# A DeltaNet and MLP-mixer kernel: every step issued in another order, with 32 products of zeros for 25

## The chip, the cores and the metric

The kernel runs on one core of a Trainium2 chip. The metric is the device time of one execution in microseconds. Before the change the median of three runs is 651.53 us (650.95 to 651.62).

## The reference

Attention in DeltaNet form for 4 batches of 8 heads, 768 time steps and head size 48, followed by an MLP mixer over time and over channels. All is fp32.

```python
k_n = k / (np.linalg.norm(k, axis=-1, keepdims=True) + 1e-06)
for t in range(S):                       # S = 768, state is D x D per batch and head
    y[:, :, t] = einsum('bhd,bhde->bhe', q[:, :, t], state)
    v_old = einsum('bhde,bhd->bhe', state, kt)
    state = state + bt * einsum('bhd,bhe->bhde', kt, vt - v_old)
# x = y as (B, S, H*D) = (4, 768, 384)
h = np.maximum(x.transpose(0, 2, 1) @ w_tok1, 0.0) @ w_tok2    # 768x256, 256x768
u = x + h.transpose(0, 2, 1)
h2 = np.maximum(u @ w_ch1, 0.0) @ w_ch2                        # 384x1536, 1536x384
return u + h2
```

## The kernel before, in words

The 768 time steps of a batch are cut into chunks of 64. A chunk is solved in closed form: the products of its keys with each other give a 64x64 triangle per head, the triangle is inverted, and the state is carried from chunk to chunk with a few products. Two chunks form a unit: 24 units u, six for each batch, 48 chunks t = 2u and 2u + 1. All work is written as Python generators, called jobs, that issue a few instructions at each step. A string named `order` lists the steps: `i0*3` means three more steps of job i0. Nothing is scheduled behind it: each engine runs its instructions in the order in which the string issues them, and waits only where an operand or a buffer is not ready. SyncE starts all the DMAs, also in that order, so a DMA that has to wait for a buffer holds back those after it.

The jobs, with a number for the unit, the round, the chunk, the batch or the piece of weights:

- w0 to w33 (`round_weights`, `round_pair`) bring in a piece of weights: step 1 is the load (L273), step 2 two ScalarE operations (L279, L280), step 3 a VectorE shift (L282), step 4 a GpSimd addition (L286). The loads share three buffers in turn, so the load of a piece waits for the GpSimd addition of the third piece before it in the list. From w22 on every second piece adds differences of weights (L301).
- k (`load_kq`) loads a unit's keys and queries, v (`load_v`) its values (last step on GpSimd, L416), b the factors beta.
- p (`prep`) scales keys and turns keys and queries on TensorE (L488, L507; from unit 12 on VectorE instead).
- c and d (`grams`) make the 64x64 products (L442) and scale them on VectorE (L445).
- t (`to_parts`) hands the 32x32 blocks on the diagonal to a round, i (`invert`) inverts a round's blocks on VectorE in some thirty small steps (L663, L668), f (`from_parts`) hands them back. Round 0 is units 0 to 3, round 1 is units 4 and 5, later rounds are four units each. Rounds 0 and 1 work on blocks of 16: L677 transposes, ScalarE (L678) and VectorE (L679) mask the two sides, L684 transposes again. From unit 6 on the blocks pass through DRAM.
- h (`join_16`, units 0 to 5) joins quarters of 16 to 32: products L701, scaling on ScalarE (L707), products L716. The first of these steps clears a buffer z on GpSimd (L543). j (`join`) joins 32 to 64: a VectorE transpose (L740), products L764, ScalarE copies (L769), products L751.
- r (`recur`) is one chunk of the recurrence: p_k on TensorE (L804), `rest` on VectorE (L811, step 5 where the state is not empty), p_y and p_w (L824, L828), a ScalarE copy (L834), p_s and p_y (L842, L843), the new state on VectorE (L851).
- m (`mixer`) is one batch of the mixer: six steps of token products (L1000), six of p_h with their additions on VectorE (L1013, L1017), then channel products (L1080 for batch 0, L972 with differences of weights for the others; L1102). s (`sum_weights`) makes those differences.
- x, z and Y (`keep_warm`, `warm_tiles`, L227 and L237) multiply zeros into a bank that nobody reads: x is 128 columns, z is 512, Y is four small ones. fp32 products take two passes on TensorE, so the profile counts each of x and z twice.

Of the kernel before, what the change touches and what calls it, by code (L numbers as in the profile page):

```python
# [23 lines left out]
def kernel(  # L24
# [1165 lines left out]
    r4*2 w16*3 p7*4 r4*2 p7 r4 j3*5 w16 p9 i1 r5*5 d7*3 w5 d7*2 c7 r5*2 c7*4 w5  # L1190
    k10*2 t6 r5*2 w5 r6*4 v3*3 w27 v3 Y v3 r5 w27 i1 w27 t6 p8*2 v4 p8*2 p7 w24*3 z
    h5*5 h4*2 r6*3 p8*2 i1 h4*3 v4 f4*2 r6*3 k11 w27 c8*5 d8*5 t7 p8 t7*2 r7*5 t7
    f4 w26*3 h4*3 p9 w26 h4 v4 h4*3 p9 j4 h4 r7*2 w24 p9*4 r7*2 p9 d9*2 p10*2 c9 f5
    c9 p9 d9*3 t6*2 r8 c9*3 Y w28 r8 j4 w28 j4*2 r7 j4 v4*2 t8*4 w4 m0 w28*2 j4*5
    w4*2 p10 f5*2 r8*2 j4 r8 h5 w27*2 w7*3 r8*2 h5*3 r8*2 w7 r9*2 h5*4 r9*2 r8 j5
# [7 lines left out]
    t10*3 r12*3 f9*2 j8*2 r13*2 j8 r13*3 w25 m0 f9*2 r13 p11 r13 p12*2 r13*2 p11  # L1203
    d11 p11 c11 w20*3 c11*2 d11 w25 c11*2 w20 d11*3 t10 p12 w30 w32*2 r14*2 w32*2
    r14 p12 r14*2 r13 v8*3 m0*3 r14 d12 v8 r14 w30*3 v8 k13*2 c12 d12 c12 w29 d12
    k13*2 w23 k13*6 c12*3 p12 d12*2 r14*2 k13 t11 k13 r14 t11 m0*3 j9 r15*4 p13*3
    m0 r15*3 p13*4 t12 w33 m0*2 t12*3 r15*3 d13 c13*2 d13*2 c13*3 d13*2 m0*3 w31*2
    j9 r16*2 j9 k14*4 r16*2 w33*4 j9*3 r16 m0 w33 w31 w33 m0 k14 r16*2 j9*3 w23*2
    r16 m0 r16 r17*2 k14*3 p14*2 t11*2 t13*4 i3 j9 v10*2 k14 p14 r17*2 r16 r17
    p14*2 k15*4 m0 v9 m0 p14 p13 v9*2 m0 i3*3 w25 v9 k14 i3 m0*2 i3 m0 i3*5 r17 k15  # L1210
    k14*2 m0*2 k15 m0*2 i3*4 r17 i3*2 r17*3 i3*6 j9 i3*2 p14 k15*2 m0*5 v9 v10
    k15*4 i3 r18*5 i3*6 m0 v10 m0 v10 m0*9 r18 d14 r18 c14 p14 d14 c14 d14*2 p15
    c14 p15*2 r18*2 m0*3 r19 c14*2 r18 f13 r19*2 f10*2 r19 p15*2 r19 m0*5 r19*2 f10
    j10 f10 f11*4 j10*2 s j10*3 j11 r19*2 d14 m0*2 k16 j11 r20*2 j11 k16*6 j11
    r20*2 j11 p15 f12 p15*2 r20 r19 t14 f12*2 k16*5 v11*2 f13*2 m0 j11 m0 r20*2
    d15*2 p16 c15 r20*3 d15 c15*3 p16*2 v11*2 c15 d15*2 t15 r21*5 p16*2 k17 m0*3
    r21 k17*2 j12*2 r21*4 p16 j12*4 j13 s r22*3 v11 r22 m0*2 r22*2 m0 p16*2 d16 r22
    c16 r22 c16 d16*3 k17 r22 c16*2 k17*7 p17*3 k17 c16 p17 r23*2 v12*4 r23*3 r22
    m0 d16 t16*2 p17 r23 p17 t16 r23 p17*2 t15*3 m0*2 t14 m0 d17 c17*3 d17 c17 d17
    s c17 d17 r23 d17 t16 s*4 m0*4 s*3 m0*3 t14 m0*3 s t14 m0 t17*4 f12 k18*2 i4*2  # L1220
    j13*2 k18*2 r23 k18*3 i4*6 j13*2 v14*2 m0*3 i4*2 m0 j13 v12 r24*2 f13 j13 r24*2
    m0 v14*2 i4*3 r24*3 k18*2 i4 k18*2 p18*2 i4 m0 i4 m0*2 i4 p18*2 i4 j13 r25*2
    j13 r25*2 p18 k19*5 r24 j13 k19*3 i4*2 m1*5 r25*2 k18 i4*2 r25 i4*4 v13*2 i4
    v13 i4 v13 m1 j13 r25*2 m1 v13 i4*4 p19 m1 p18*3 k19*4 r25 m1*2 r26*3 f16 r26
    p19*2 m1 r26 m1*3 s r26*2 c18 d18 c18 d18*2 p19 m1*3 r26*3 m1*3 f14 m1*2 r27*2
    c18 r27*3 p19 f14*3 c18 d18*2 m1*2 j14 r27*2 c18 m1 r27 j14*2 f15*2 p19 j14*3
    m1*2 p19*2 f15*2 j15*2 r27 r28*2 j15 v14 f16*2 s r28*3 j15 r27 j15 j16 k20 s*3
    j15 m1*2 k20 m1 k20*10 m1*2 r28*2 d19 c19*2 d19 c19 d19 c19 d19*2 r28*2 c19 t18
# [19 lines left out]
    r42*2 j22 m2*4 j22 m2*3 r43*2 f22 r43 r42 r43 m2*3 r43 m2*12 f23 m2*3 r43 m2
    r43 j23 m2*2 r43*3 j23*3 r44*3 j23*2 r44 v22*2 r44 m2*5 r44*2 m2*3 r44*3 m2*3
    f23 m2*4 r45 j23 r45*3 j23*3 r45*3 m2*7 r45 v23 m2*4 v23 m2*2 v23 m2*2 v23  # L1250
# [39 lines left out]
```

## Time and profile before

| what | value |
|---|---|
| median of 3 runs | 651.53 us |
| profiled execution, its own time | 652.18 us |
| its span, first to last instruction | 650.4 us |
| TensorE busy | 619.6 us (95%) |
| VectorE busy | 446.4 us (69%) |
| ScalarE busy | 259.6 us (40%) |
| GpSimd busy | 108.6 us (17%) |
| mean granted TensorE clock | 0.976 |
| DMA | 50.25 MB, 75 GB/s of HBM traffic over the span |

Times in the views are microseconds from the span's start. PE is TensorE, PEld its weight loads, DVE VectorE, ACT ScalarE, POOL GpSimd, SP SyncE. A row of the timeline has the start, the duration, the engine, the line, the operation, output and inputs, and in brackets the engine's idle time before it and what ended it. Digits of the page's second part are busy shares of 40 equal slices in tenths.

### The profile page before, as it was taken

What the parts mean: (1) busy time and instruction counts of PE and PEld (TensorE: products, weight loads), DVE (VectorE), ACT (ScalarE), POOL (GpSimd) and SP (SyncE); (2) the same over time, 40 slices, a digit from 0 to 9 for tenths busy, and PEclk for the clock granted to TensorE, in tenths of its full rate; (3) what the DMA queues carried; (4) which work ended last, traced back from release to release, by engine and by line L of the source; (5) the groups of instructions that cost most, each with busy time, mean ns of one, the idle gap of its engine ahead of it and who ended that gap; (6) DMA issues with size and microseconds to landing.
All of it is one profiled execution on the core that took longest, in us unless ns stands there. A gap on an engine that the chain in (4) does not pass through costs nothing.

```text
span 650.4 us, 21453 instructions
## 1 busy us (share of the span) xinstructions
PE 619.6 (95%) x9116; PEld 537.1 (83%) x9116; DVE 446.4 (69%) x1132; ACT 259.6 (40%) x631; POOL 108.6 (17%) x147
## 2 busy tenths in 40 slices
PE   7669989799999999999999999999999999999997
...
PEclk9977989899999999999999999999999999999999
...
GB/s 179 143 136 103 152 136 125 169 176 117 132 115 68 87 88 98 114 66 114 95 67 128 70 41 61 59 17 37 21 30 17 26 3 0 25 1 25 2 25 24
DMA packets 135776, 50.25 MB, mean 77 GB/s; under 512 B 114657, under 2 KB 130145, under 8 KB 135681
## 3 DMA queue, kind: packets, MB, share of 16 engines
...
q14 instruction: 25, 0.20, 0.1%
...
## 4 chain that ended last, share of the span: by engine, by line
PE 71%; SPq 2%; DVE 1%; issue 1%; ACT 1%; DMA 1%; DVEq 0%; ACTq 0%
PE p_o L1102 25%; PE p_r L972 18%; PE p_c L1080 7%; PE p L1000 4%; PE p_h L1013 4%; PE p_k L804 2%; PE p_y L824 2%; PE p_g L442 2%; PE p_s L842 2%; PE p_z L764 2%; PE p_ut L1023 1%; PE p_y L843 1%; PE p_w L828 1%; SPq L359 1%; PE p_x L751 1%
## 5 line engine op out<-in xcount | busy, mean ns | idle before, releaser
L1102 PE MATMUL p_o<-wc,r 128*128 128x192 f32 x720 | 127.2, 329 | 0.6 <-ACT u_t L1027 0.6
L1102 PEld LDWEIGHTS p_o<-wc,r 128*128 128x128 f32 x720 | 116.7, 190 | 3.1 <-ACT u_t L1027 1.1
L984 DVE TENSOR_TENSOR r<-r,p_r 128x512 f32<-128x512 f32 x90 | 60.1, 685 | 42.2 <-PE p_r L972 40.1
L1031 DVE TENSOR_TENSOR xb<-xb,p_o 128x192 f32<-128x192 f32 x84 | 29.3, 351 | 55.9 <-PE p_o L1102 55.4
L981 ACT COPY r<-p_r 128x512 f32<-128x512 f32 x54 | 31.5, 585 | 87.8 <-PE p_r L972 87.8
L668 DVE TENSOR_TENSOR x<-x,sub 128x84 f32<-128x84 f32 (+24 forms) x178 | 60.9, 342 | 6.1
L663 DVE TENSOR_TENSOR sub<-x 128x84 f32<-128x84 f32 (+24 forms) x178 | 57.7, 324 | 7.6 <-DMA x<-n_dram 3.5
L416 POOL TENSOR_TENSOR v_st<-v_st,nrm 128x384 f32<-128x384 f32 x24 | 20.8, 866 | 183.0 <-DMA v_st<-in_v_dram 129.9
L1102 PE MATMUL p_o<-wc,s 128*128 128x192 f32 x288 | 50.6, 330 | 0.3 <-DVE xb L1031 0.3
L1080 PE MATMUL p_c<-u_t,wc 128*128 128x256 f32 x216 | 50.7, 386 | 0.0
L1102 PEld LDWEIGHTS p_o<-wc,s 128*128 128x128 f32 x288 | 46.8, 190 | 1.2 <-DVE xb L1031 0.6
L856 ACT ACTIVATE xb<-p_y 64x192 f32<-64x192 f32 x96 | 31.1, 324 | 36.4 <-PE p_y L843 22.6
L988 ACT ACTIVATE r<-r 128x512 f32<-128x512 f32 x54 | 34.0, 630 | 26.5 <-DVE r L984 26.2
L1080 PEld LDWEIGHTS p_c<-u_t,wc 128*128 128x128 f32 x216 | 39.8, 190 | 5.7 <-ACT u_t L1027 0.3
L442 PE MATMUL p_g<-kq 48*64 48x128 f32 (+1 forms) x704 | 34.4, 281 | 6.0 <-ACT kq L511 5.8
L499 POOL TENSOR_TENSOR mb<-mask_c,cs 128x512 f32<-128x512 f32 x20 | 21.1, 1053 | 113.1 <-DVE cs L478 74.1
L972 PE MATMUL p_r<-u_t,wc 128*128 128x128 f32 x288 | 38.5, 277 | 0.0
L834 ACT COPY w_t<-p_w 128x192 f32<-128x192 f32 x48 | 15.3, 318 | 57.9 <-PE p_w L828 56.9
L972 PE MATMUL p_r<-t_d,wc 128*128 128x128 f32 x288 | 36.8, 280 | 0.0
L972 PEld LDWEIGHTS p_r<-u_t,wc 128*128 128x128 f32 x288 | 35.4, 192 | 0.3
L442 PEld LDWEIGHTS p_g<-kq 48*64 48x64 f32 (+1 forms) x704 | 25.5, 135 | 12.0 <-ACT kq L511 6.9
L286 POOL TENSOR_TENSOR wc<-w_f,d 128x384 uint32<-128x384 uint32 x24 | 24.8, 1038 | 59.7 <-ACT d L280 23.5
...
## 6 DMA issues: line engine op xcount, KB each, us to landing
d<-in_moe_w_ch_dram SPq DMA_DIRECT2D x24, 384.0 KB, 3.7
v_st<-in_v_dram SPq DMA_DIRECT2D x96, 48.0 KB, 2.6
...
kst<-in_k_dram SPq DMA_DIRECT2D x64, 48.0 KB, 2.9
...
pads<-in_k_dram SPq DMA_DIRECT2D x24, 96.0 KB, 2.5
pads<-in_q_dram SPq DMA_DIRECT2D x24, 96.0 KB, 2.6
...
```

Of the source, the lines that this page charges most:

```text
L442: nc.tensor.matmul(p_g[PAR[i ^ cc], p], kqt[f, p, cc, 0], kqt[f, p, cc])
L663: nc.vector.tensor_tensor(out=tmp, in0=y[:, :, 0:s, s : s + 1].to_broadcast([n, k, s, w]), in1=y[:, :, s : s + 1, s + 1 : m].to_broadcast( ...
L668: nc.vector.tensor_tensor(out=y[:, :, 0:s, s + 1 : m], in0=y[:, :, 0:s, s + 1 : m], in1=tmp, op=ALU.add,)
L856: nc.scalar.mul(y[:, :, D * i : D * i + D], p_y[PAR[1 - i]], 1.0 if c else -1.0)
L972: nc.tensor.matmul(p[:, i], pieces[i // width][:, at : at + 128], f[f"u{n}"], start=first and i == 0, stop=True, skip_group_check=True,)
L981: nc.scalar.copy(o, p)
L984: nc.vector.tensor_tensor(out=o, in0=o, in1=p, op=ALU.add if sign > 0 else ALU.subtract)
L988: nc.scalar.activation(o, o, ACTF.Relu)
L1000: nc.tensor.matmul(p_1[dh], piece_of(w1, c, 0)[:, dh * 128 : (dh + 1) * 128], xb[:, c], start=(c == 0), stop=(c == NCH - 1),)
L1031: nc.vector.tensor_tensor(out=xb[:, c, e], in0=xb[:, c, e], in1=p, op=ALU.add)
L1080: nc.tensor.matmul(p_c[:, k], piece_of(wc1, cb, f * 128)[:, f * 128 : (f + 1) * 128], u_t[:, cb], start=(cb == 0), stop=(cb == NCB - 1),)
L1102: nc.tensor.matmul(p, a[:, m], wc2[:, m, j], start=(start and i == 0), stop=(i == NM - 1), skip_group_check=True,)
```

## The change

Only the string `order` differs. It lists the same steps of all jobs in another sequence; of the products of zeros there are 11 x, 17 z and 4 Y where there were 8, 14 and 3. The code of the jobs is untouched. Three cuts follow: the start up to the first recurrence steps, the stretch from r9 to r12, and the end.

```diff
@@ the start
-    t3*3 p4*3 i0*3 v0*2 p4*4 d4*2 v0 c4*2 z i0*2 d4 i0 w1 v0 i0*8 k6*2 k7*2 k5*2
-    k6*2 z i0 w18*3 w1 c4*3 i0 k6 p6*2 p4 p6 z w6*2 d4*2 z*2 w6 h1*3 t4*3 i0 h1*2
-    p5 h0*5 p5 k8 p5*2 h2*4 v0 f0*3 w8*2 k7 w17*4 z h0*3 f1 k8 f1*2 h0*5 j0 k8*3 z
-    k8 p8*2 w6 j0 h2 j0*3 f2*2 h1*3 j0 h1*5 p6 w8*2 f2 j0*5 j1 p5*6 v1*3 r0*5 h2*4
...
+    c3 d3 k4 c3 t1*2 p4 d3 x w18 c3 t1 t2 w18*2 w8 d3 c3 d3 k5 v1*2 d3 p4*2 k5*2 t0
+    c3 t2*2 t3*2 k7 p4 w1 t3 i0 p6 i0 p6*2 p4*2 i0*7 k8 z p4*4 v1 c4 k8 w6 d4 w1
+    c4*4 d4*2 w8 w6 i0*2 d4 z v0*2 i0*3 x k8 z*3 w1 i0*2 d4 x w17*3 t4 z h0*4 i0
+    k5*2 h1*2 k8 h1*2 h0 h1 w17 z f0*3 h0 w8*2 p3 v1 h0 p5 f1*3 k8 h0*3 v1 v0 h0*2
+    v0 h2*3 t4 h2 h0 z f2 h2 w0*2 j0 w11 j0 w6 j0*4 k5 h1*6 j0*3 h1*2 f2*2 j1 p5 t4
+    v0 j0*2 w6 p5*6 h2 p5 r0 w14 h2*2 r0*4 h2*4 c5*4 k7 k9 h2 r0*2 p8 p5 j1 c5 j1*2
...
@@ from r9 to r12
-    p10 v5*2 p10 r9*4 j5*2 w4 m0 j5*2 t9*4 i2*4 m0 w15*2 j5 i2*2 z r9 r10 x i2*3 r9
-    r10 w22 r10 w15*2 i2 v5*2 i2*4 j5*2 x w29*2 j5 w29 x i2 v5 r10*2 w29 j5 i2 v6*2
-    w12 i2*2 w22 j5 r10*2 k11*3 p10*2 w12*2 i2 p10*2 r10*2 m0 r11 k11*2 i2 w12 r11
-    r10 w22*2 w19*3 r11*3 w19 c10*2 i2 d10*2 i2*4 p11 i2 p11 r11*2 i2*4 x k12*4 v6
-    r11*2 k12 m0 k12 m0*2 k12*2 w25 w31*2 v7*4 k12*4 w21 v6*2 i2*2 m0*3 v7 m0 p11*2
-    m0*3 p10 f6 w27 f6 w21 p12 w21 d10*3 p12*2 f6*2 f7*3 j6 c10*2 w31*2 c10 w25*3
-    m0*2 f8*3 m0 j6*5 f7 m0 j7*6 m0 p11*3 r12*2 w21 w29 r12*3 f8 j8*3 w29 w23*4
...
+    r9*2 i2 w29 j5 p10*2 r9 j5 i2*3 j5 w29 w12 k11*2 k12 j5 r9 i2 k11 v7 m0 r9 w15
+    r10 j5*2 i2 j5 w12 w29 r10*2 i2 w19 i2 r10 p10 m0 p10 w19 k11*2 r9 v5 w12*2 k12
+    d10*2 i2 w22 j5 d10 j5 r10*2 x i2 d10 i2 r10 w19 Y r10 i2*2 m0 w29 r10 w19 z
+    w21 Y p11 k12 r11 r10 w31 Y i2 w22*2 r11*3 k12 i2*2 r11 i2 m0 r11 i2*2 w22 v7*2
+    c10 w31 r11*2 c10*2 i2 k12*2 r11 m0 x i2*4 v7 k12 i2*4 x z w25 v6*2 m0 i2*2 v6
+    k12*2 v6 k12 i2 f6 m0*2 c10 m0 f6*3 w25 m0 c10 m0 w21 w25*3 f7 m0*2 p11 w21*2
+    w23 f7 m0*2 w27 d10 m0 p11 j6 v6 j6*4 p10 f7 w31*2 f7 w30 f8*3 p12 j6 j7 p12
+    w29 w23 t10 w29 w23 f9 m0 w25 j7 p12 j7*4 f8 m0 p11*3 r12*3 p12 r12 f9 r12 w23
...
@@ the end
-    r45*2 m2*13 j23 r46*4 v23 r46 m2*11 r46*2 m2*6 r46*3 m2*3 r47*5 m2*6 r47 m3*4
-    r47*3 m3*2 m2*4 m3*6 m2 m3 m2*6 m3*5 m2*6 m3*156
+    m2*2 r45 m2*3 r46*5 m2*5 j23 m2*12 r46*2 m2 r46*3 m2*4 r47*4 m2*4 r47*3 m2*6
+    r47 m2*5 m3*4 r47 m2*2 m3*2 m2 m3*7 m2*12 m3*2 m2 m3*159
```

More of the change, by code (lines that the diff above doesn't have):

```diff
@@ L1190 @@
[L1190 to L1195, printed above, removed]
@@ L1202 @@
-    m0*2 f8*3 m0 j6*5 f7 m0 j7*6 m0 p11*3 r12*2 w21 w29 r12*3 f8 j8*3 w29 w23*4
[L1203 to L1228, printed above, removed]
@@ L1248 @@
[L1248 to L1252 removed]
+    w10 z w10*2 z k1 z b k0 k1*2 b z x k1*2 k3 k0 z k1 k0*2 p1*2 k0 w2 k0 p0*2 b p1
+    p0 w10 p0*7 p1*3 k3*2 w2 d0 w2 c0 k2*2 c0 w18 d0*3 k3 w2 c0*3 d0 k3 p1*3 c1*2
@@ new lines @@
+    v0 j0*2 w6 p5*6 h2 p5 r0 w14 h2*2 r0*4 h2*4 c5*4 k7 k9 h2 r0*2 p8 p5 j1 c5 j1*2
+    r0 k7 r1*2 k7 k9 r1 k9 w0*2 r1 d5*3 r1 k9 w11*3 d5*2 j1 r1 w14 p6*2 w9 p8 v2 j1
+    h3*2 t5 j2 r1 p6 h3*2 f3 r1 k9*2 h3 j1*2 w14 j1*3 k7 p6 t5*2 r1*2 r2*3 w9 r2 x
+    j2*3 i1*2 w14 j2*2 p6 r2*2 w16 r2 p6 f3*2 h3 i1*4 k10 r2*2 h3 i1 h3 d6 h3 p6 r2
+    r3*2 d6 r3 d6 r3 i1 v2 x i1 h3*4 r3 d6 v2*2 w16 c6*2 w9 c6*2 k10 d6 c6 p7 w16
+    p7 r3 j3 j2*2 r3 p7 r3*2 j2*2 j3 w9 j3 r4*2 k7 v3 p7 r4*2 j2 r3 j3*2 v2 j3 w16
@@ new lines @@
+    r4 k10 p7*2 w24 v3 r4*2 k10 i1*2 t6 i1 w5 p7*2 r4 w27 p7 j3*4 r4*2 d7 i1 r5 i1
+    r5 i1 r5 j3 k8 v3*2 d7 r5*2 d7*3 k10 w5 c7*3 r5 w27 w5 v4 r5 w5 c7*2 r5 p8*3
+    r5*2 r6*4 w24 v4 t7 i1 z p8*4 p9 v3 r6 h5 w27 h5 v4*2 h5*3 r6*2 w26 h4*2 t7 d8
+    h4 w24 i1 h4*2 t7 d8*3 r6 w24 w27 t7 c8*4 t6*2 f4*3 d8 h4*3 p9 w26 p9 r6 r7 k10
+    r7 r6 h4 p8 c8 w28 t6 h4*3 v4 r7*2 h4 w7 p9 r7 p9*2 r7 p9*2 r7*2 p9 c9 w26 w28
+    j4 d9 c9 w26 k11 c9*2 f5 p10 w28*2 d9*3 r7 c9 r8*2 w7 t8*2 d9 r8*2 j4*2 p10 t8
@@ new lines @@
+    j4*2 w7 j4 p7 p10 t8 v5 m0 f5 p10 p9 f5 v5 j4*3 w4 w15 w4 r7 t9*2 w4 j4*2 t9*2
+    h5 w15 z r8*2 h5*2 v5 h5 v5 r8*2 w27 w7 w4 w15 Y r8 r9*4 h5*3 r8 p10 h5 i2 j5*2
+    r9*2 i2 w29 j5 p10*2 r9 j5 i2*3 j5 w29 w12 k11*2 k12 j5 r9 i2 k11 v7 m0 r9 w15
+    r10 j5*2 i2 j5 w12 w29 r10*2 i2 w19 i2 r10 p10 m0 p10 w19 k11*2 r9 v5 w12*2 k12
+    d10*2 i2 w22 j5 d10 j5 r10*2 x i2 d10 i2 r10 w19 Y r10 i2*2 m0 w29 r10 w19 z
+    w21 Y p11 k12 r11 r10 w31 Y i2 w22*2 r11*3 k12 i2*2 r11 i2 m0 r11 i2*2 w22 v7*2
@@ new lines @@
+    c10 w31 r11*2 c10*2 i2 k12*2 r11 m0 x i2*4 v7 k12 i2*4 x z w25 v6*2 m0 i2*2 v6
+    k12*2 v6 k12 i2 f6 m0*2 c10 m0 f6*3 w25 m0 c10 m0 w21 w25*3 f7 m0*2 p11 w21*2
+    w23 f7 m0*2 w27 d10 m0 p11 j6 v6 j6*4 p10 f7 w31*2 f7 w30 f8*3 p12 j6 j7 p12
+    w29 w23 t10 w29 w23 f9 m0 w25 j7 p12 j7*4 f8 m0 p11*3 r12*3 p12 r12 f9 r12 w23
+    j8*2 f9 w30 t10 w23 r12 j8*3 r12*2 r13*3 j8 v7 w30 r13*2 m0 r13*2 p11 w32 p12
+    p11*2 r13 t10 w20 s*2 k12 w30 w20 k12 v8 c11 w32 d11 c11 d11 r13 r14 t10 d11
+    w31 r13 k13 c11 r14 w20 c11 w20 w23 d11 c11 d11 p12*2 r14*3 k13 m0*3 v8 w32 r14
@@ new lines @@
+    w32 k13*2 d12 c12*2 d12 c12 d12 c12*2 k13 w25 d12*2 p12 w31 r14*4 k13*2 m0*2
+    w27 w23 k13 r15*2 w29 k13*2 r15 j9 p11 p13 r15*2 p13 m0 p13*2 k13 p13 k13 p13
+    r15 p13 m0*3 v8 w33 v8 d13 c13 t12 d13 c13 d13 c13 d13 c13 t11 r15*2 p13 r15
+    t11*2 d13 c13 m0*2 t11 w33 r16*2 t12 r16 f9 t12 k14 r16 k14 j9*2 k14*2 w33*2 v8
+    r16 j9*3 k14*2 m0*2 k14*2 m0 t13 m0 r15 t13 w33 r16 w33 p14*2 j9*2 t12 r16*3
+    w33 r16 w31 m0 r17 p14*2 t13 j9 r17*2 j9 r17 p14 r17 t13 i3*2 k14 i3 m0*2 r17
+    k14 v10 k15*2 i3*3 p14 i3 m0 k14 m0 i3 k14 v10 p14 i3*3 m0*2 i3 m0 k15*2 m0 r17
```

72 lines of the change are left out of this document (44 added, 28 removed).

## The prediction

> **What bounds the kernel now.** I read the page first, then the windows, then the queues of VectorE, GpSimd and SyncE inside the windows where TensorE is not full. From the page:
>
> ```profile
> span 650.4 us, 21453 instructions
> ...
> PE 619.6 (95%) x9116; PEld 537.1 (83%) x9116; DVE 446.4 (69%) x1132; ACT 259.6 (40%) x631; POOL 108.6 (17%) x147
> ...
> PE   7669989799999999999999999999999999999997
> ...
> PEclk9977989899999999999999999999999999999999
> ```
>
> TensorE is busy for 619.6 of 650.4 us, and the slices that are not full, and those with a lowered clock, lie in the first nine. The windows put sizes on it (PE, PEld, DVE, ACT, POOL busy; granted clock; DMA):
>
> ```profile
> 20.00:40.00 20.00, 14.17 (x127) 8.42 (x126) 17.34 (x47) 9.89 (x25) 4.88 (x6) 0.83 0.72 142
> 40.00:60.00 20.00, 13.78 (x200) 9.54 (x198) 14.12 (x31) 11.49 (x30) 10.14 (x13) 0.66 0.40 92
> 120.00:140.00 20.00, 15.75 (x222) 10.64 (x221) 19.04 (x43) 9.12 (x24) 8.01 (x9) 0.83 0.62 145
> 158.41:600.00 441.59, 439.78 (x6365) 392.70 (x6365) 307.42 (x778) 149.08 (x351) 45.86 (x62) 1.00 0.26 61
> ```
>
> From 158.41 (the first product of recurrence step r12) to 600 TensorE idles 1.8 us in 441.6. The products themselves are the same in both orders, so the time is: when r12 starts, plus products that do not change, plus whatever new holes the order makes. Holes that can be closed lie before 158: 20:40 (5.8 us idle), 40:60 (6.2) and 120:140 (4.3). So I follow the new order up to r12 and ask how much earlier r12 comes.
>
> **The first inversion and the first join (20 to 62 us).** VectorE's queue here, in order:
>
> ```profile
> 31.97 1.98 DVE L655 STREAM_TRANSPOSE x<-r 128x1024 f32<-128x1024 f32 x1
> ...
> 44.51 2.86 DVE L679 TENSOR_SCALAR r<-r,even 128x512 f32<-128x512 f32 x1 [0.79 <-ACT r L678]
> 47.29 0.53 DVE L468 TENSOR_REDUCE ksum<-ksq 128x8 f32<-128x384 f32 x1
> 47.75 0.67 DVE L445 TENSOR_TENSOR gm<-p_g,mb 128x512 f32<-128x512 f32 x1
> 48.94 0.36 DVE L282 TENSOR_SCALAR w_f<-d 128x384 uint32<-128x384 uint32 x1 [0.52 <-issue]
> 49.84 0.38 DVE L601 COPY r<-gm 32x256 f32<-32x256 f32 x1 [0.55 <-ACT r L598]
> 50.24 2.02 DVE L684 STREAM_TRANSPOSE r<-x 128x1024 f32<-128x1024 f32 x1
> ```
>
> and what stands beside the slow L679, with its two runs, TensorE's wait for it, and the step that uses L684's output:
>
> ```profile
> 44.62 2.01 POOL L543 MEMSET z<- 128x2304 f32 x1
> L679 DVE TENSOR_SCALAR r<-r,even x2: 489/1674/2858, 44.5 to 93.3; 128x512 f32<-128x512 f32 x2
> 47.52 1.77 PE L701 MATMUL p_z<-r,wc 64*64 64x32 f32 x29 [5.87 <-DVE r L679]
> 53.17 0.72 ACT L621 ACTIVATE wc<-r,even 128x256 f32<-128x256 f32 x1
> ```
>
> 1. *L679.* The same instruction took 2.858 us beside GpSimd's memset of z and 0.489 us in the second round. In the old order the memset is queued behind w18's and w1's additions and p4.10; in the new one w18's addition comes before t0's copy, and the memset follows w1's addition, which I place near 38, so it ends near 41.4, before L679 can start (about 43.8). Gain 2.4 us; bounds 0 (the memset slips onto it again) and 2.4. The Trainium skill (SBUF — State Buffer, "Who interferes with whom") says that whichever of the two engines starts first holds the shared ports and the other blocks; here L679 is recorded 0.11 us ahead of the memset and is still the one that is long, so the recorded start does not tell who held them. By the rule as written this term would be 0 and the sum 2.4 us higher.
> 2. *Start of i0.* The load of k0 is issued one load (0.6 us) earlier, and VectorE's and GpSimd's queues between unit 3's square root and i0 are shorter by my count (7.2 us for 8.0); together -1.4 us. Against it, p6.2 now stands behind i0.2, and its loads behind w1's, which waits for w18's addition: +0.9 us. Net -0.5, bounds -2 and +1.
> 3. *From L679 to L684.* In the old order 2.9 us pass (47.37 to 50.24). In the new one only d4.5 (0.67) and w17.3 (0.36) stand between: 1.0 us. Gain 1.9. Then f0.1 follows at once instead of 0.9 us later behind p5.3 (53.17 against 52.26): gain 0.8.
> 4. *A new wait.* p5.8 (transposes of unit 5's queries) now stands on TensorE ahead of r0.1. Its load k5.6 is queued on SyncE behind w0.1 and w11.1; w11.1 needs the buffer that w6's GpSimd addition frees, and that is now behind v1.5, f2.3, t4.3 and v0.5.
>
> ```profile
> d<-in_moe_w_ch_dram SPq DMA_DIRECT2D x24, 384.0 KB, 3.7
> kst<-in_k_dram SPq DMA_DIRECT2D x64, 48.0 KB, 2.9
> pads<-in_q_dram SPq DMA_DIRECT2D x24, 96.0 KB, 2.6
> 61.81 0.81 PE L828 MATMUL p_w<-v_st,wc 64*64 64x48 f32 x15
> ```
>
>    With 2.6 us for that load, I get w6's addition at 54.0, w11 issued to 54.4, k5.6 to 55.0, landed at 57.6; TensorE would be ready near 56. Behind p5.8 wait h2.6 and r0. About 2.1 us of the gain goes.
>
> Sum at r0.1: -2.4 - 0.5 - 1.9 - 0.8 + 2.1 = -3.5 us, that is 58.3 instead of 61.81.
>
> **The recurrence up to r9 (62 to 114).** The windows give what the engines did up to r9.5:
>
> ```profile
> 0.00:114.12 114.12, 93.59 (x1922) 71.52 (x1922) 76.33 (x204) 78.95 (x211) 47.99 (x68) 0.90 0.67 140
> ```
>
> Counted step by step with the durations of before (neighbours overlap in the record, so VectorE's and ScalarE's sums are some per cent above their busy time) and without the products of zeros, the work ahead of r9.6 is 71.5 and 71.7 us on TensorE, 79.6 and 79.6 on VectorE, 87.1 and 88.2 on ScalarE. The order inside is different but no engine is given more; I take the gain on unchanged, -3.5 to -4 (bounds -6 and 0).
>
> **The round of units 6 to 9 (114 to 143).** Here VectorE is the bound:
>
> ```profile
> 114.12:143.34 29.22, 24.33 (x336) 15.89 (x334) 26.54 (x70) 12.78 (x32) 8.01 (x9) 0.88 0.67 169
> 121.91:127.42 5.51, 1.82 (x46) 1.37 (x40) 5.24 (x11) 0.82 (x3) 2.21 (x4) 0.86 0.65 143
> 127.91 0.31 PE L828 MATMUL p_w<-rest,gm 64*64 64x48 f32 x1 [4.18 <-DVE rest L811]
> 142.79 0.55 DVE L1017 TENSOR_TENSOR xb<-xb,p_h 128x384 f32<-128x384 f32 x1
> ```
>
> r10.5 (rest, L811) stands behind i2.11 to i2.15 and one rounding, the 5.5 us of the second row, and TensorE waits 4.18 us. In the new order these five steps come after r10.5, so that wait goes. But what is late next is the same VectorE: m0.7's addition of p_h (142.79) has i2.2 to i2.29 ahead of it in both orders, and the fourth p_h product needs it. VectorE's work from r9.5 to the end of that addition, summed step by step, is 28.2 us before and 26.8 after (w15's rounding, p11.2 and i2.30 move out), so of the 4.18 us only about 1.6 (0 to 4.2) is kept. At the fourth p_h product: -3.5 to -4 less 1.6, say -5.6.
>
> **From there to r12.** VectorE has less room after than before:
>
> ```profile
> 143.34:156.60 13.26, 13.20 (x155) 9.89 (x156) 9.18 (x21) 5.37 (x13) 6.72 (x8) 1.00 0.50 115
> 156.60 0.45 DVE L740 STREAM_TRANSPOSE t<-gm 128x256 f32<-128x256 f32 x1 [0.30 <-DMA gm<-w_dram]
> ```
>
> In 13.26 us it has 9.18 us of work, and the transpose for j8 ends 13.7 us after m0.7's addition. In the new order 3.7 us more stand ahead of r12 (w25.5, p11.4, p12.4, w25.6), and f7's loads are behind w23's load, which waits for a GpSimd addition. I place j8's transpose 17.4 us after the addition. TensorE reaches j8.2 after 15.9 us, and r12.6 is now behind j8.2: +1.8 us (0 to 4). So r12 is 3.8 us earlier.
>
> **The products of zeros.** Their durations and one at the low clock:
>
> ```profile
> L227 PE MATMUL p_warm<-warm x44: 275/593/1222, 1.1 to 135.3; 128*128 128x512 f32 x28, 128*128 128x128 f32 x16
> 33.48 2.08 PE L227 MATMUL p_warm<-warm 128*128 128x512 f32 x2
> ```
>
> Three more of z, three more of x, one more of Y: with two passes each and the longest pass of the first row, 1.222 us, 17 us; with the middle one, 0.593, 8 us. All stand before m0.7, where TensorE waits for VectorE, loads or ScalarE (5.8 + 6.2 + 4.3 us in the windows above), so I cost them at nothing; if that cover is gone they cost about 5 us: three z at half of 2.08, four short ones at two passes of 0.275.
>
> **After r12.** Per step of the recurrence the work on each engine stays within some us of the old order; VectorE is 1 to 4 us further ahead in the list than TensorE between r12 and r23. New holes: 0 (0 to +4). The tail, mixer m3 alone on TensorE, is issued in the same sequence: 0.
>
> **Sum.** -3.8 us on the profiled execution's 652.18 us (span 650.4): 648.4. It lies 0.65 us above the median of the runs, 651.53, so the median becomes 647.7.
>
> **Rivals.**
> *All of the early gain is kept* (chance 0.20). k5.6 or j8's transpose do not hold TensorE: neither 1.8 nor part of the 2.1 is lost, -6.4 us, 645.1. For it: landing times of loads spread, and 2.6 is a median; against it, both waits follow from the order of a queue.
>
> *The zeros stand in the way* (0.14). z.7 to z.11 and two of x come in a row before the first join. At the low clock of the row at 33.48 five z take 10.4 us instead of 5, and the join waits some 4 us: -3.8 + 4.2, 651.9, no change. It decides if the gap on TensorE ahead of p4.8, whose load is behind w1's, lowers the clock; I count 2.7 us for it. In the trace the clock was 0.53 in this stretch after a gap of 4.02 us:
>
> ```profile
> 30.00:35.00 5.00, 2.60 (x18) 1.25 (x18) 3.99 (x10) 2.80 (x7) 1.87 (x2) 0.53 0.61 105
> 32.41 1.15 PE L442 MATMUL p_g<-kq 64*64 64x128 f32 x16 [4.02 <-ACT kq L511]
> ```
>
> The Trainium skill (TensorE: Matmul & The Clock Gate, "The HAM clock gate") puts the idle window that halves the clock at about 3.4 us, free-running. The two gaps fall on either side of it; by that rule alone this rival would not happen, yet the window's phase leaves it open.
>
> *Slower: VectorE is the bound up to j8* (0.24). i2's load is pinned by the chain grams, DRAM, load, and does not come earlier, so only the 1.4 us of moved work are gained at m0.7; then j8's transpose is late, and GpSimd's additions w25, w21, v6, p10 and w31, now in the same stretch, lengthen VectorE's two-input operations, as here, where one of L668's nearly equal operations took 1.07 us and another 0.39:
>
> ```profile
> 120.80 1.07 DVE L668 TENSOR_TENSOR x<-x,sub 128x198 f32<-128x198 f32 x1
> 123.66 0.39 DVE L668 TENSOR_TENSOR x<-x,sub 128x220 f32<-128x220 f32 x1
> ```
>
> Five times 0.68 is 3.4 us: -1.4 + 1.8 + 3.4 = +3.8, 655.3. It decides if r9's subtraction is not earlier than 113 and j8's transpose ends over 17 us after m0.7's addition. Against it: the work up to r9 is equal and starts earlier.
>
> **How the numbers follow.** Forecast 647.7 with chance 0.42, the rivals 0.20, 0.14 and 0.24. About 0.2% (1.3 us) is what a measurement of this kernel can tell from no change. Faster by more: 0.42 + 0.20 = 0.62. Within: 0.12 of the zeros' 0.14. Slower: 0.24 + 0.02 = 0.26. The range leaves out a tenth on each side: 643.5 below (the second case with 1.6 us more from the round of units 6 to 9), 655.5 above (the third rival's time). The forecast's own range is 644.5 to 650.5.
>
> **What would show it.** Right: L679 near 0.5 us; L684 by 46; r0.1 near 58 with a wait for kq or p_t just ahead of it; no 4 us wait of L828 on L811 near 125; m0.7's addition near 137; r12 near 154.6. Wrong: r0.1 at 61 or later; a wait of some us of L764 on L740 near 155; or idle time of over 4 us between r12 and 600.

## The result and the profile after

| what | before | after |
|---|---|---|
| median of 7 runs each | 651.53 us (650.19 to 652.02) | 647.15 us (643.65 to 647.66) |
| profiled execution, its own time | 652.18 us | 647.63 us |
| its span | 650.4 us | 645.9 us |
| mean granted TensorE clock | 0.976 | 0.987 |

The ratio is 0.9921, interval 0.9896 to 0.9945: faster by 0.8%. Run again beside other kernels, the new order gave 644.83 us (641.78 to 647.34) against 651.85, ratio 0.989 (0.9867 to 0.9914). Its thirteen runs spread over 5.9 us, with 645.16 in the middle. The seven runs of before in the table spread over 1.8 us, but its runs beside the experiments over 4.6 to 9.4, so the new order is not alone in its scatter. One run of old_to_r12_then_new (below), 671.77 us at a granted clock of 0.959, fell into a slower state of the chip and is left out of that kernel's median and range. The profile of after is one of its longer executions; the profile of the second time (below: new_again) has a span of 640.0.

The page of after, the same rows as the prediction showed of before:

```profile
span 645.9 us, 21493 instructions
...
PE 615.6 (95%) x9136; PEld 533.2 (83%) x9136; DVE 446.8 (69%) x1132; ACT 259.9 (40%) x631; POOL 109.0 (17%) x147
...
PE   8589888999999999999999999999999999999997
...
PEclk8979979999999999999999999999999999999999
```

TensorE is busy 4.0 us less although it runs 20 passes more: its products took less time each, because the clock fell less. The windows say where (PE, PEld, DVE, ACT, POOL busy; granted clock; DMA):

```profile
20.00:40.00 20.00, 12.56 (x126) 8.46 (x127) 18.59 (x50) 11.28 (x29) 11.03 (x12) 0.83 0.83 171
40.00:60.00 20.00, 18.07 (x439) 14.22 (x438) 13.93 (x29) 17.18 (x46) 11.51 (x15) 1.00 0.45 101
120.00:140.00 20.00, 19.44 (x190) 12.02 (x186) 17.96 (x48) 6.63 (x17) 1.83 (x2) 1.00 0.46 122
150.50:280.00 129.50, 126.35 (x2080) 111.00 (x2080) 97.39 (x242) 41.75 (x109) 23.28 (x28) 1.00 0.42 97
```

In 40:60 the clock is 1.00 where it was 0.66, and 439 products run where 200 ran; 120:140 has 0.6 us of idle time for 4.3. The last row, from the start of r12, has new holes: 3.15 us idle in 129.5, where before had 0.63 in the 126.6 us behind its own start of r12 (158.40 to 285). The rows around the first inversion:

```profile
29.49 1.95 DVE L655 STREAM_TRANSPOSE x<-r 128x1024 f32<-128x1024 f32 x1
...
42.30 0.49 DVE L679 TENSOR_SCALAR r<-r,even 128x512 f32<-128x512 f32 x1 [0.79 <-ACT r L678]
...
43.57 2.05 DVE L684 STREAM_TRANSPOSE r<-x 128x1024 f32<-128x1024 f32 x1
```

```profile
37.74 2.02 POOL L543 MEMSET z<- 128x2304 f32 x1
```

```profile
33.94 2.47 PE L442 MATMUL p_g<-kq 64*64 64x128 f32 x32 [3.83 <-ACT kq L511]
36.34 6.19 PE L227 MATMUL p_warm<-warm 128*128 128x512 f32 x14
42.93 2.06 PE L701 MATMUL p_z<-r,wc 64*64 64x32 f32 x64 [0.40 <-DVE r L679]
```

The memset of z is over at 39.76, so L679 is short; L684 follows 0.78 us after it; and TensorE waits 0.40 us for L679 instead of 5.87, with 6.2 us of zeros ahead of it.

The account of the time, from the starts of five steps in each trace (us): i0.1 is the first step of the inversion of round 0 (L655), r0.1, r12.6 and r24.1 are products of the recurrence, and the last column ends where m3's last product (the last 18 passes of L1102) starts.

| kernel (by its label) | i0.1 | r0.1 | r0.1 to r12.6 | r12.6 to r24.1 | r24.1 to m3's last |
|---|---|---|---|---|---|
| before | 31.97 | 61.81 | 97.69 | 115.99 | 368.84 |
| after | 29.49 | 53.56 | 98.09 | 119.99 | 368.14 |
| new_again | 28.49 | 52.51 | 95.09 | 118.52 | 367.80 |
| new_to_r0_then_old | 29.81 | 53.88 | 97.51 | 115.54 | 368.85 |
| new_to_r12_then_old | 28.42 | 52.49 | 95.30 | 115.52 | 368.85 |
| new_old_r12_to_r24_new | 28.46 | 52.50 | 96.32 | 118.84 | 368.08 |
| old_to_r12_then_new | 32.82 | 62.61 | 102.06 | 120.76 | 367.68 |
| new_no_zeros_first_join | 29.73 | 58.48 | 98.95 | 118.62 | 368.25 |

So the new start with its zeros brings 8 to 9 us, the middle 2.6 at the best and -0.4 in after, and the stretch from r12 to r24 takes 2.5 to 4 back. The 0.7 to 1.0 us less behind r24 are no gain: the new list has one step of m0 ahead of r24.1 that the old one has behind it (234 passes of L1102 between r12.6 and r24.1 for 228), and six such passes take 1.0 us (36 of them took 6.01). With both columns added up, the new list loses 1.5 (new_again) to 3.6 us behind r12.

### The profile page after: what moved, and what is told of

Read it like the earlier page. It is cut to its first block, busy times and chain, and to the rows that moved or that the text cites. A ratio compares the mean times of both kernels' runs of the same rounds, so it can differ in the third digit from the quotient of the medians.

```text
span 645.9 us, 21493 instructions
## 1 busy us (share of the span) xinstructions
PE 615.6 (95%) x9136; PEld 533.2 (83%) x9136; DVE 446.8 (69%) x1132; ACT 259.9 (40%) x631; POOL 109.0 (17%) x147
## 5 line engine op out<-in xcount | busy, mean ns | idle before, releaser
L1102 PE MATMUL p_o<-wc,r 128*128 128x192 f32 x720 | 126.3, 329 | 0.9 <-ACT u_t L1027 0.6
L1102 PEld LDWEIGHTS p_o<-wc,r 128*128 128x128 f32 x720 | 116.7, 190 | 3.0 <-ACT u_t L1027 1.1
L668 DVE TENSOR_TENSOR x<-x,sub 128x84 f32<-128x84 f32 (+24 forms) x178 | 58.9, 331 | 6.1
L1080 PE MATMUL p_c<-u_t,wc 128*128 128x256 f32 x216 | 51.3, 387 | 1.3 <-ACT r L1089 0.7
L1102 PE MATMUL p_o<-wc,s 128*128 128x192 f32 x288 | 51.2, 330 | 0.3 <-DVE xb L1031 0.3
L1102 PEld LDWEIGHTS p_o<-wc,s 128*128 128x128 f32 x288 | 46.8, 190 | 1.2 <-DVE xb L1031 0.6
L1080 PEld LDWEIGHTS p_c<-u_t,wc 128*128 128x128 f32 x216 | 39.6, 190 | 7.4 <-ACT r L1089 1.1
L442 PE MATMUL p_g<-kq 48*64 48x128 f32 (+1 forms) x704 | 37.5, 285 | 7.8 <-ACT kq L511 6.2
L442 PEld LDWEIGHTS p_g<-kq 48*64 48x64 f32 (+1 forms) x704 | 26.8, 136 | 12.0 <-ACT kq L511 7.3
L972 PEld LDWEIGHTS p_r<-t_d,wc 128*128 128x128 f32 x288 | 34.1, 191 | 1.1 <-DVE r L984 0.2
```

The lines of the kernel that those rows point to most:

```text
L442: nc.tensor.matmul(p_g[PAR[i ^ cc], p], kqt[f, p, cc, 0], kqt[f, p, cc])
L668: nc.vector.tensor_tensor(out=y[:, :, 0:s, s + 1 : m], in0=y[:, :, 0:s, s + 1 : m], in1=tmp, op=ALU.add,)
L972: nc.tensor.matmul(p[:, i], pieces[i // width][:, at : at + 128], f[f"u{n}"], start=first and i == 0, stop=True, skip_group_check=True,)
L1080: nc.tensor.matmul(p_c[:, k], piece_of(wc1, cb, f * 128)[:, f * 128 : (f + 1) * 128], u_t[:, cb], start=(cb == 0), stop=(cb == NCB - 1),)
L1102: nc.tensor.matmul(p, a[:, m], wc2[:, m, j], start=(start and i == 0), stop=(i == NM - 1), skip_group_check=True,)
```

## The experiments

My theory was that the gain comes from the start, and that the new list loses some of it behind r12; the rival, that whoever reaches r12 8 us earlier loses some of it again, whatever the list behind.

**The two lists cut at r12.** The first kernel has the new list up to r12 and the old one from there, the second the reverse; each takes the other list's remaining steps in their order.

```diff
 new_to_r12_then_old
-    p11*3 r12*3 p12 r12 f9 r12 w23 j8*2 f9 w30 t10 w23 r12 j8*3 r12*2 r13*3 j8 v7 w30
+    p11*3 k12*2 v7 w27 p11 r12*5 j8*3 w23 t10*2 r12*3 f9 j8*2 r13*2 j8 r13*3
...
 old_to_r12_then_new
-    p11*3 r12*2 w21 w29 r12*3 f8 j8*3 w29 w23*4 t10*3 r12*3 f9*2 j8*2
+    p11*2 w25 w21 w23 w30 w29 w23 t10 w29 w23 f9 w25 f8 r12*3 p12 r12 f9 r12 w23 j8*2 f9
```

> The new order up to the first step of r12, then the remaining steps in the old order. In the two profiles r12 starts at 158.41 and 150.50, 7.9 us earlier with the new order, and from there to the end the new order's TensorE idles 8.2 us and the old one's 5.4. Theory A, the two parts are independent: the new order wins 7.9 us before r12 and loses about 3.4 after it by holes of its own (the waits near 185 to 200 and at 252.6). Then this kernel keeps the 7.9: 651.5 - 7.9 = 643.6 us, and the hole before L442 on L368 near 250 is gone. Rival B, whoever comes to r12 8 us earlier runs into loads or VectorE and gives 3 us back whatever the order: 647.

Measured: 641.50 us (639.47 to 645.19), ratio 0.9849 (0.9821 to 0.9878). That is 2.1 us below the theory's 643.6; in its profile r12.6 comes at 147.79, 3.9 us earlier than in after under the same list.

> The old order up to the first step of r12, then the rest in the new order. Theory A (the new order's later part has holes of its own): r12 near 158.4 and 3 to 3.4 us lost after it, 651.5 + 3.4 = 654.9 us, slower than both. Rival B (the loss comes from being early): 651.5 us, no change.

Measured: 660.90 us (655.65 to 663.32), ratio 1.0116 (1.008 to 1.0153), 6 us above what I expected. With the old list behind r12 the last two columns add up to 484.4, as in the kernel before (484.8); with the new list they take 486.3 in new_again, 488.1 in after and 488.4 here. The loss belongs to the new list behind r12, whatever came ahead. Of the rest, 4.4 us lie between r0.1 and r12.6, where j8's transpose (L740) starts only at 163.84 and holds r12.6: a wait that neither list has by itself.

The longest wait of TensorE behind r12 is seen in the rows of TensorE, of VectorE and of ScalarE in after:

```profile
254.11 1.15 PE L442 MATMUL p_g<-kq 48*64 48x128 f32 x32 [1.54 <-DVE kq L368]
```

```profile
250.40 0.55 DVE L468 TENSOR_REDUCE ksum<-ksq 128x8 f32<-128x384 f32 x1 [2.87 <-ACT ksq L465]
251.62 0.20 DVE L477 RECIPROCAL ksum<-ksum 128x8 f32<-128x8 f32 x1 [0.67 <-ACT ksum L474]
252.04 2.02 DVE L368 STREAM_TRANSPOSE kq<-pads 128x512 f32<-128x512 f32 x2
```

```profile
249.84 0.52 ACT L465 ACTIVATE ksq<-kst 128x384 f32<-128x384 f32 x1 [4.04 <-DMA kst<-in_k_dram]
```

The last load of unit 17's keys is started by 247.38, since five other DMAs now stand among its loads on SyncE, and the products of its keys follow 6.7 us later: the chain of load, square, sum, root, reciprocal and transpose fills all of that, and TensorE waits for its end. In the old list 8.8 us lie between the same two points (248.86 and 257.62), and the last transpose is over at 256.48, 1.1 us before the products start. Of the 4.0 us that r12.6 to r24.1 takes longer in after, 2.4 are idle time of TensorE (3.0 us for 0.6: this wait, and waits of 0.3 to 0.7 us between 165 and 202 us at L1080, L842 and L1102, which I have not traced further). The other 1.6 are more work in that stretch, 1.0 of it the step of m0.

**The old list from r12 to r24 only.**

```diff
 new_old_r12_to_r24_new: up to r24 as new_to_r12_then_old, then
+    m0*3 i4*2 m0 j13 v12 i4*2 f13 m0 k18 i4 r24*4 k18*2 j13*3 k18 r24*3 v14 i4 m0 i4 m0
```

> The new order up to r12, the old order from r12 to r24, the new order from r24 on. Theory: all of the loss behind r12 lies between r12 and r24 (120.0 us from r12.6 to r24.1 in the new order, 116.0 in the old one, 115.5 with the new start), and from r24.1 to the last product of the mixer the new order is 0.7 us shorter (368.1 against 368.8). So r12.6 to r24.1 takes 115.5 to 116, the rest 368.1, and the median is 3 to 5 us below the new order's, about 0.7 us below that of the new order to r12 with the old one behind. Rival: the joint at r24 costs it (steps that the two lists have in another order wait, 1 to 3 us), and r24.1 to the end takes 369 us or more.

Measured: 643.44 us (638.85 to 646.86), ratio 0.9866 (0.9833 to 0.9899). From r24.1 on it took 368.08, as expected. From r12.6 to r24.1 it took 118.84 where I had expected 115.5 to 116. Of this, 1.0 us is the step of m0 that the joint puts ahead of r24.1. For the rest, a load for i3 came late in this execution (VectorE), and TensorE waited for an addition behind it:

```profile
185.80 0.19 DVE L663 TENSOR_TENSOR sub<-x 128x30 f32<-128x30 f32 x1 [3.72 <-DMA x<-n_dram]
```

```profile
188.36 2.22 PE L1102 MATMUL p_o<-wc,r 128*128 128x192 f32 x12 [1.96 <-DVE xb L1031]
```

In new_to_r12_then_old the same wait for x was 0.18 us. So the 0.7 us that I had taken for a gain behind r24 is a step counted in the other column, and no run shows a gain there; 643.44 and the 644.83 of the new order beside it are not told apart by their intervals.

**The new start alone.**

```diff
 new_to_r0_then_old
-    p5 t4 v0 j0*2 w6 p5*6 h2 p5 r0 w14 h2*2 r0*4 h2*4 c5*4 k7 k9 h2 r0*2 p8 p5 j1 c5 j1
+    p5*4 h2 p5 k7*3 k8 p8*2 p6 p5 r0*5 h2*3 k7 p7 r0 h2*3 c5 h2 c5*2 r0 r1*2 p7 c5*2
```

> The new order up to the first recurrence step r0, the old order from there. Theory: the start alone brings 8 us at r0.1 (53 against 61.8), and the old list from r0 to r12 gives half of it back, since its loads and VectorE's rounds do not come earlier by as much; r12.6 then starts near 154, and the time is 644 to 648. Rival 1: all 8 us are kept through r12, r12.6 at 151.5, and the time is near 643. Rival 2: the old middle needs the old start; less than 2 us are kept, 649 to 651.

Measured: 644.07 us (642.80 to 645.60), ratio 0.9884 (0.9865 to 0.9902). My theory fell and the first rival held: r12.6 starts at 151.39, and r0 to r12 takes 97.51 us against 97.69 before, so all of the 7.9 us are kept. The new start with the old rest is as fast as the whole change, and its six runs lie within 2.8 us.

**The memset and L679.** In the old list a new step q clears z earlier; in the new list z is cleared three times.

```diff
 old_early_clear
-    t3*3 p4*3 i0*3 v0*2 p4*4 d4*2 v0 c4*2 z i0*2 d4 i0 w1 v0 i0*8 k6*2 k7*2 k5*2
+    t3*3 p4*3 i0*3 v0*2 p4*4 q d4*2 v0 c4*2 z i0*2 d4 i0 w1 v0 i0*8 k6*2 k7*2 k5*2
...
 new_three_clears
-            nc.gpsimd.memset(borrowed["z"], 0.0)
+            for _ in range(3):
+                nc.gpsimd.memset(borrowed["z"], 0.0)
```

> The old order with one thing changed: GpSimd's memset of z is issued right after p4.7, where GpSimd stood idle from 33.07 to 42.19, not after p4.10. Theory: L679 falls from 2.86 to 0.49 us and h0, f and r0 come about 2.4 us earlier; carried on to the end as the new order carried its early gain (7.9 of 8.25 at r12), 651.5 - 2.3 = 649.2 us. Rival: the chain behind it has slack, the gain goes into the wait for ScalarE and w6's shift that follow L679 (2.9 us between L679 and L684), or into the 4 us wait at r10: 651.5 us with L679 at 0.5 us all the same.

Measured: 648.86 us (648.23 to 649.12), ratio 0.9951 (0.9935 to 0.9968).

> The new order, with z cleared three times in a row instead of once, so that GpSimd is busy with memsets from 37.7 to about 43.8 and L679, which started at 42.30, stands beside one. Theory: L679 takes 1.5 to 2 us instead of 0.49 and all behind it is 1.0 to 1.5 us later: 648.5 us or so. If the ports are held by the one that starts first, L679 has to wait for the end of the memset in progress. Rival: memsets that only write do not disturb L679, which stays near 0.5 us; then the time is that of the new order, 647.2, and the 2.86 us in the old order came from another instruction, p4.10 for one.

Measured: 649.02 us (645.23 to 654.33), ratio 0.996 (0.9929 to 0.9991). L679's two runs, by its line, in the first and in the second kernel (there one line lower), and the three memsets:

```profile
L679 DVE TENSOR_SCALAR r<-r,even x2: 485/696/907, 44.8 to 91.5; 128x512 f32<-128x512 f32 x2
```

```profile
L680 DVE TENSOR_SCALAR r<-r,even x2: 487/1189/1891, 41.2 to 87.5; 128x512 f32<-128x512 f32 x2
...
36.66 6.17 POOL L544 MEMSET z<- 128x2304 f32 x3
```

In the old list the first of L679's two runs falls from 2.86 us to 0.91, not to the 0.49 expected, and the time falls by 2.5 us: GpSimd's memset of r still stands beside it (44.94 to 45.47, L679 44.84 to 45.75). In the new list a longer memset makes it 1.89 us again: it starts at 41.21 and ends at 43.10, 0.27 us behind the last memset (42.83). In the kernel before, L679 started at 44.51 while GpSimd was busy with p4.10's operation (L516), and it ended at 47.37, 0.28 us behind the memset of r, which follows that of z:

```profile
43.85 0.82 POOL L516 TENSOR_TENSOR gm<-kst,cs 128x384 f32<-128x384 f32 x1
44.62 2.01 POOL L543 MEMSET z<- 128x2304 f32 x1
46.57 0.52 POOL L576 MEMSET r<- 128x512 f32 x1
```

So in all three kernels GpSimd was at work when L679 started (in the first with L516 again, from 44.17 to 45.00), and L679 ended 0.27 or 0.28 us after the last of GpSimd's memsets. In the second kernel r0.1 comes at 53.87 where runs with the same i0.1 have 52.5: 1.4 us, as expected.

**The products of zeros ahead of the first join.** Left out are seven products that nobody reads.

```diff
 new_no_zeros_first_join
-     w6 i0*2 d4 z v0*2 i0*3 x k8 z*3 w1 i0*2 d4 x w17*3 t4 z h0*3
+     w6 i0*2 d4 v0*2 i0*3 k8 w1 i0*2 d4 w17*3 t4 h0*3
```

> The new order without seven products of zeros ahead of the first join (z.7 to z.11 and two of x, 36.3 to 42.5 us in its profile). Theory of the prediction: they lie where TensorE waits for L679, which ends at 42.8 either way, so taking them away gives no time: the median stays within 1 us of the new order's, or is up to 2 us slower where the granted clock falls after the longer gap. Rival (the zeros stand in the way): the join starts up to 1 us earlier and the time falls by 1 us or more.

Measured: 650.34 us (645.03 to 654.15), ratio 0.9975 (0.9947 to 1.0003): without these seven the gain cannot be told from nothing. The products do not stand in the way; by the medians they carry more than half of the gain, and leaving them out costs more than the 2 us that I had allowed for the clock. TensorE and its clock without them, and the clock of the new order in three of the same windows:

```profile
35.00:40.00 5.00, 1.64 (x24) 1.24 (x20) 4.55 (x17) 1.00 (x3) 3.15 (x3) 0.50 0.74 183
45.00:50.00 5.00, 5.00 (x68) 3.43 (x68) 4.17 (x6) 2.94 (x7) 3.48 (x6) 0.50 0.33 82
50.00:55.00 5.00, 5.00 (x62) 3.43 (x60) 1.06 (x3) 3.05 (x9) 3.06 (x6) 0.50 0.34 92
```

```profile
35.00:40.00 5.00, 5.00 (x30) 2.92 (x27) 4.53 (x17) 1.00 (x2) 3.15 (x3) 0.62 0.77 187
45.00:50.00 5.00, 4.34 (x78) 2.69 (x79) 4.80 (x8) 4.70 (x12) 3.64 (x5) 1.00 0.31 74
50.00:55.00 5.00, 4.46 (x149) 4.00 (x146) 2.25 (x6) 4.68 (x15) 3.88 (x7) 1.00 0.49 113
```

```profile
43.15 3.62 PE L701 MATMUL p_z<-r,wc 64*64 64x32 f32 x64 [6.51 <-DVE r L679]
```

Without the zeros the gap of 6.51 us is followed by half the clock up to 55 us, though TensorE is busy all the time from 45 to 55; the join's first 64 products take 3.62 us for 2.06, and r0.1 comes at 58.48, which is 4.7 us later after a start of i0 0.24 us later. In the kernel before L701 took 3.63 us after its gap of 5.87: it paid the same.

**The products of zeros from 119 to 131 us.** Eight are left out, twice, the second time beside the new order itself (new_again).

```diff
 new_no_zeros_units_6_to_9
-     d10 j5 r10*2 x i2 d10 i2 r10 w19 Y r10 i2*2 m0 w29 r10 w19 z w21 Y p11 k12 r11 r10
-    w31 Y i2 w22*2 r11*3 k12 i2*2 r11 i2 m0 r11 i2*2 w22 v7*2 c10 w31 r11*2 c10*2 i2
-    k12*2 r11 m0 x i2*4 v7 k12 i2*4 x z w25 v6*2
+     d10 j5 r10*2 i2 d10 i2 r10 w19 r10 i2*2 m0 w29 r10 w19 w21 p11 k12 r11 r10 w31 i2
+    w22*2 r11*3 k12 i2*2 r11 i2 m0 r11 i2*2 w22 v7*2 c10 w31 r11*2 c10*2 i2 k12*2 r11 m0
+    i2*4 v7 k12 i2*4 w25 v6*2
```

> The new order without eight products of zeros between 119 and 131 us (three of x, two of z, three of Y). Theory: they lie in TensorE's waits for VectorE's i2, so the median stays within 1 us of the new order's, and m0.7's addition starts within 0.5 us of where it started relative to r9.5. Rival 1: they delay m0.7 to m0.10 (two of x and a z end at 131.3), and the time falls by 0.5 to 1.5 us. Rival 2: without them the granted clock falls to 0.5 to 0.8 in 120:135 and the time rises by 1 to 3 us.

> The new order without eight products of zeros between 119 and 131 us, on the same chip as the new order. Theory: the 642.7 of the first time came from r4 to r9, ahead of these products, and r9.5 to m0.10 took 27.7 us against 27.2 with them; so they are worth nothing, and the median is within 1.5 us of the new order's here. Rival: they cost 2 us or more, and the median is again that much lower than the new order's.

Measured: 642.66 us (641.41 to 643.43, four runs), ratio 0.9858 (0.9828 to 0.9888), and then 644.07 (642.52 to 651.68), ratio 0.9901 (0.9862 to 0.994), against 644.83 and 0.989 of the new order beside it. The first time looked like a gain, but in its trace what was earlier lay ahead of these products (r9.5 at 103.32 for 108.25). Side by side no difference is seen in the times, and from r9.5 to r12.6 the traces take 43.9 and 43.0 us without the eight for 43.4 (after) and 43.8 (new_again) with them: in these traces they are worth less than 1 us, either way.

**The scatter of the new order.** From r4.1 to r9.5 after takes 35.2 us, new_again 31.7. In after SyncE took 2.35 us over the start of one DMA, the loads of two pieces of weights behind it came late, and ScalarE waited for them ahead of the copy that TensorE needs:

```profile
74.33 2.35 SPq L610 DMA_DIRECT2D n_dram<-gm  x1
```

```profile
79.95 0.44 ACT L279 ACTIVATE d<-d 128x256 f32<-128x256 f32 x1 [1.05 <-DMA d<-in_moe_w_tok_dram]
81.15 0.55 ACT L279 ACTIVATE d<-d 128x384 f32<-128x384 f32 x1 [0.44 <-DMA d<-in_moe_w_ch_dram]
82.15 0.32 ACT L834 COPY w_t<-p_w 128x192 f32<-128x192 f32 x1
```

I moved the two pieces behind that copy, in the new order and in the one with the old list from r12, and ran the new order again beside other kernels.

```diff
 new_w5_behind_r5 (and, with the same edit, new_to_r12_then_old_w5)
-    r5 i1 r5 j3 k8 v3*2 d7 r5*2 d7*3 k10 w5 c7*3 r5 w27 w5 v4 r5 w5 c7*2 r5 p8*3
-    r5*2 r6*4 w24 v4 t7 i1 z p8*4 p9 v3 r6 h5 w27 h5 v4*2 h5*3 r6*2 w26 h4*2 t7 d8
+    r5 i1 r5 j3 k8 v3*2 d7 r5*2 d7*3 k10 c7*3 r5 v4 r5 w5 w27 c7*2 r5 p8*3
+    r5 w5*2 r5 r6*4 w24 v4 t7 i1 z p8*4 p9 v3 r6 h5 w27 h5 v4*2 h5*3 r6*2 w26 h4*2 t7 d8
```

> The new order with one edit: ScalarE's and VectorE's operations of two pieces of weights (w5 and w27) stand behind r5.7 (ScalarE's copy of w_t, L834) and r5.9 instead of ahead of them. Theory: in the profiled run of the new order SyncE's start of a DMA took 2.35 us just ahead of these two loads, ScalarE waited 1.05 and 0.44 us for them in front of r5's copy of w_t, TensorE waited 2 to 3 us for that copy and then ran at a granted clock of 0.50 up to 90 us; this is the 3 us between the two levels of the new order's times (643.7 to 644.5, and 647.2 to 647.7). With the two pieces behind r5, all runs come near 644 us, 80:90 us has clock 1.00 and r9.5 starts near 105.5. Rival: the levels have another cause (the slow starts of DMAs fall on other loads too, or the clock itself differs); then both levels stay, the median is within 1 us of 647.2, and the profile of an upper run has its loss at another place.

> The new order up to r12, the old order from there, with the pieces w5 and w27 behind r5.7 and r5.9 as well. Theory: the two gains add up; runs of the kernel without the second edit were at 639.5 to 645.2 with a median of 641.5; with it they come together near 640. Rival: the scatter has another cause, and median and spread stay as they were.

> The changed kernel itself once more, beside the three others on the same chip. Theory: its runs again lie in two levels, near 644 and near 647.5, because r4 to r9 take 32 to 33 us in some executions and 35 to 36 in others. Rival: one level near 647 only, and what was below came of the chip of that day.

Measured: 645.26 us (642.61 to 648.57), ratio 0.9902 (0.9868 to 0.9936); 643.73 (642.01 to 647.71), ratio 0.9888 (0.9853 to 0.9924); and 644.83 for the new order. The spread stays, and in the first one's profile r9.5 comes at 108.46 where I had expected 105.5, so this theory fell. In new_again ScalarE even waited 0.85 and 0.43 us for the same two loads, and that execution is among the shortest. In the ten profiles that have the new list from r0 to r12, with or without the edits above, the stretch takes 94.8 to 98.95 us. It goes with the clock: the mean granted clock of the stretch is 0.98 to 1.00 in the five that take 94.8 to 97.0 us and 0.95 to 0.97 in the five that take 97.1 to 98.95. Which waits lower the clock in one execution and not in another stays open. The other half of what I expected of new_again, two levels, did not hold either: its six runs lie at 641.8, 643.3, 644.5, 645.2, 645.6 and 647.3.

## Why the prediction was right, and where not

Forecast 647.7, measured 647.15. The direction is right, and the size comes of errors that cancel: up to r0.1 8.25 us were gained where 3.5 had been forecast, and of the 4.75 us more, 0.7 was lost on the way to r12 and 3.3 behind it, where nothing had been forecast. That it came so close is luck in the draw as well: over the thirteen runs of the new order the middle is 645.16. The sum itself has a slip, too: it takes 4.0 us into the round of units 6 to 9 where its own terms add up to 3.5, which makes the forecast 0.5 us too low.

- **L679** (forecast -2.4): 2.86 to 0.49 us, -2.37. Moving the memset of z alone brought 1.95 of it in old_early_clear, and lengthening it in new_three_clears took 1.4 back. In the new list the memset ends 2.5 us before L679 starts, so the two do not meet, and the rule of the Trainium skill (SBUF — State Buffer, "Who interferes with whom"), by which this term would have been 0, was not put to a test there. I had also read the rows of before wrongly for it: I compared L679 with the memset alone, but GpSimd was ahead, with L516. With three memsets, too, GpSimd starts first and VectorE lasts until it is done, as the rule says. What the rule, told for one instruction, does not say is that L679 waited through several of GpSimd's in a row: in before through the rest of L516 and two memsets.
- **L679 to L684, f0.1 at once** (-1.9 and -0.8): L679's end to L684's start is 0.78 us for 2.87 (-2.1), and L684 to f0.1 2.09 for 2.93 (-0.8). Right.
- **Start of i0** (-0.5): 2.48 us earlier in after, 2.1 to 3.7 in the eleven profiles with the new start. Mis-sized by 2 us: the wait of p6.2 (0.9) that I set against the gain did not come; it ran at 31.81 with no idle time before it. The other 1.1 us I have not traced. The eleven fall into two groups: i0.1 is at 28.3 to 28.5 in seven and at 29.5 to 29.8 in four, and in just these four the clock is 0.50 from 8.5 to 11.5 us, where it is 1.00 in the seven. So 1 us of the scatter is there before the first inversion starts.
- **The new wait for k5.6** (+2.1): the step that failed. The load started at 48.55 and p5.8 ran at 52.81 without a wait. I took each load of a weight to need the buffer of the third piece before it; the trace shows it start right after the addition that comes first in the list: w0's load at 44.84 behind w17's addition, w11's at 48.17 behind w8's. The kernel's description ahead of the prediction is wrong in this, too.

```profile
44.84 0.33 SPq L273 DMA_DIRECT2D d<-in_moe_w_tok_dram  x1
48.17 0.33 SPq L273 DMA_DIRECT2D d<-in_moe_w_ch_dram  x1
48.55 0.55 SPq L385 DMA_DIRECT2D pads<-in_q_dram  x1
```

```profile
43.78 1.03 POOL L286 TENSOR_TENSOR wc<-w_f,d 128x384 uint32<-128x384 uint32 x1 [4.03 <-DVE w_f L282]
...
46.94 1.21 POOL L286 TENSOR_TENSOR w<-w_f,d 128x384 uint32<-128x384 uint32 x1 [0.36 <-DVE w_f L282]
```

- **The zeros** (0): the other failed step. I priced what they cost, which is indeed nothing, and not what they save: seven of them keep the clock, worth 4.7 us at r0.1 by the experiment. They are why the way from f0.1 to r0.1 is shorter (7.90 us for 8.64) and not longer: without them it takes 11.15 (47.33 to 58.48). The trace of before had the number: clock 0.66 in 40:60 behind the gap of 5.87 us.
- **r0 to r12** (r9 carried, -1.6, +1.8): 97.69 us before, 98.09 in after, 95.1 in new_again. The wait of L828 on r10.5 is gone (127.42 to 116.88), and the one I feared at j8 did not come: its transpose ended 15.5 us behind m0.7's addition, not 17.4. Of the gain in the round of units 6 to 9 after keeps little, because 2.7 us had been lost up to r9, where the gain was to be carried unchanged; from r9.5 to the end of m0.7's addition the gain is 2.5 us for the 1.6 forecast, and from there to r12.6 0.2 us are lost for 1.8.
- **After r12** (0, up to +4): +3.3 in after, at the upper end, and +1.5 in new_again. I compared work per engine, which is equal; the largest hole found there comes of how long ahead of its use a load is started.

Of the rivals, the zeros in the way fell by experiment, in the opposite direction. The low clock that it supposed did come: the gap of 2.39 us ahead of p4.8, for which I had counted 2.7, was followed by one of 3.83, and the clock was 0.50 in 36:38. But the zeros were over at 42.53, before L679 was (42.79). The early gain kept whole came true (new_to_r0_then_old), at 8 us instead of 6.4. The slower case did not come: r9.5 was at 108.25, not behind 113.
